# A hand-ordered kernel on one core: the opening fifth in another order, with alpha of chunk 0 loaded first

## The chip, the core and the metric

The kernel runs on one core of one Trainium2 chip. A core has four compute engines: TensorE (PE, matrix products and transposes into PSUM), VectorE (DVE), ScalarE (ACT) and GpSimd (POOL). A fifth one, SyncE (SP), here only issues the DMA transfers. Each engine works through a queue of its own in order, and waits on semaphores for what other engines or DMAs produce. The metric is the device time of one execution in microseconds (us); lower is better.

## The reference

```python
def _attn_ref(q, k, v, alpha):               # each (4, 8, 768, 48)
    for t in range(S):
        state = alpha[:, :, t, :, None] * state + np.einsum('bhd,bhe->bhde', k[:, :, t], v[:, :, t])
        y[:, :, t] = np.einsum('bhd,bhde->bhe', q[:, :, t], state)

x = attn_out.transpose(0, 2, 1, 3).reshape(3072, 384)
h = x @ w_in                                 # 384 x 2048
g = h * np.clip(h + 3.0, 0.0, 6.0) / 6.0
out = g @ w_out                              # 2048 x 384
```

The first half is a gated linear attention: a state of 48 x 48 per batch and head is decayed by alpha and updated at each of 768 positions. The second half is a feed-forward block with the hard-swish activation on the 3072 tokens. The two weight matrices come as float64.

## The kernel before

**Tiling.** The sequence is cut into chunks of 128 positions: 6 chunks for each of 4 batches, 24 in all, numbered j. Two chunks form a group g of 256 tokens. In a chunk the recurrence is turned into matrix products: products of alpha along the chunk scale k and q, and scores inside halves of 64 positions, together with a state carried between the halves, give y.

**Steps.** The program is a list of short words. Each word names a step and its arguments, and `run` calls them in the written order; each step's instructions go to the queue of their engine in that order. Nothing else sets the order. The words used below:

- `la.j`, `lk.j`, `lq.j` (line 251 for j under 6, line 262 from 6 on): SP loads alpha, k, q of chunk j. Up to chunk 5 they go into three ring buffers `rings`; from 6 on each load is four DMAs into the tiles `aq`, `kq`, `qq` (Python name `quads`), whose 16 padding columns are set by two POOL memsets (line 257) at the first use of each tile. `lv.j.z` (272): two DMAs that load v into buffer z.
- `w.i` (162, 166): SP loads slice i of the weights as float64, 768 KB, i from 0 to 7 of the first matrix and 8 to 15 of the second. `d1.i` (186), `d2.i` (196), `dx.i` (191) on ScalarE, `d3.i` (203, 205, or 207 to 210) on VectorE and `d4.i` (217) on POOL turn it to float32. Slices share five raw buffers: slices 0, 5, 8, 11, 14 the first, 1, 6, 9, 12, 15 the second, 2, 7, 10, 13 the third, 3 and 4 one each. A later load into a buffer waits for the `d4` of the earlier slice.
- `ta.j`, `tk.j`, `tq.j` (282): PE transposes into a PSUM bank (from chunk 6 on VectorE does it, 286). `ca.j` (300): copy of alpha, ScalarE. `r.j` (309, 313) and `p.j` (320): VectorE scans that give decay and growth. `k.j`, `q.j` (332): the scaled k and q.
- `kb.j` (374, PE) and `ck.j` (378, ACT): k by token. `u.j` (429, PE), `sm.j.b` (437, 439, DVE), `st.j` (409, POOL): the state. `sv.j.b` (419 on ACT; 415 on POOL where a batch starts), `qa.j.b` (366, ACT): state and q placed beside v and scores. `sc.j` (346, PE), `m.j` (356, DVE): scores and mask. `ya.j`, `yb.j` (455, PE), `cy.j` (464, ACT): y of both halves, kept as `xT`.
- `fa.i`, `fb.i` (489) and `f.g.i` (478): PE, hidden block i of group 0 in halves, or of a whole group; `fr` (494, ACT) and `fg` (498, DVE) apply the activation. `b.c.n` (516, PE): the second product for chunk c.
- `x`, `y` (537 to 541, 647), `xc`, `s`: VectorE sums of weights and inputs, with which groups from 2 on use fast matrix multiplication: `M.g.i` (600, PE) are products of the first matrix, `P.g.i` (703, PE) of the second, from group 1 on. `O`, `so`: stores, SP. `K`, `G`, `n`, `o`, `e`, `h`: copies and sums behind them.
- `z.m.n` (532): n matmuls of the identity on PE whose result nobody reads.

Each DMA of the SP queue waits, besides its buffers, for the eighth DMA before it. So at most eight are under way, and the loads follow each other in the order of their words.

Of the kernel before, what the change touches and what calls it, by code (L numbers as in the profile page):

```python
# [17 lines left out]
def kernel(  # L18
# [228 lines left out]

    def load_akq(name, j):
# [6 lines left out]
        if j < FIRST + NQ:  # L255
            for o in (BLK, 3 * BLK):
                nc.gpsimd.memset(to[o : o + BLK, :, V - 1, D - BLK : BLK], 1.0)
# [675 lines left out]
```

## Time and profile before

| | us |
|---|---|
| median of 3 runs | 534.24 (534.19 to 534.98) |
| the profiled execution, its time | 533.84 |
| its span in the profile | 531.8 |
| PE busy | 522.2 (98%) |
| DVE busy | 477.0 (90%) |
| ACT busy | 257.4 (48%) |
| POOL busy | 50.4 (9%) |

Times in a profile count from the start of the span. A row of a timeline has the start, the time from its first instruction's start to its last one's end, the engine, the line of the kernel, the operation, the tiles out<-in with shapes, the count of instructions, and in brackets the idle time of the engine before it with what ended it. A float32 matmul has two records, and the records of a row overlap: 24 records of 128x256 at line 478 take 5.45 us in one row, so 0.23 us each. A row of stretches has the length and then, for each engine, the busy time and the number of instructions, the granted TensorE clock, the mean busy share of the 16 DMA engines (sums of packet times, which can exceed 1) and GB/s. In a list of DMA issues the last column is the time from issue to landing.

### The profile page before, as it was taken

Reading aid. Unit: us, or ns where it says so; the run is one execution under the profiler, and the core shown is the slowest. Engines: PE = TensorE matmul, PEld = TensorE weight load, DVE = VectorE, ACT = ScalarE, POOL = GpSimd, SP = SyncE. Lnnn points to the kernel's source line nnn. Section 1 sums busy time; section 2 is a strip of 40 time slices with the busy share of each in tenths; the row PEclk is TensorE's granted clock in tenths of the full one; section 3 lists DMA queues with packets and bytes.
Section 4 is the critical chain, followed back from the end, with each engine's and each line's share of the span. In section 5 each row is a group of like instructions: output and inputs, shape, how many; then the busy total and the mean of one; then the engine's idle time right before and its main releaser. Section 6 shows DMA issues by size and latency. Waiting matters only on the chain.

```text
span 531.8 us, 15143 instructions
## 1 busy us (share of the span) xinstructions
PE 522.2 (98%) x6306; PEld 496.9 (93%) x6306; DVE 477.0 (90%) x849; ACT 257.4 (48%) x503; POOL 50.4 (9%) x71
## 2 busy tenths in 40 slices
...
DMA packets 124100, 54.40 MB, mean 102 GB/s; under 512 B 83328, under 2 KB 116864, under 8 KB 124032
## 3 DMA queue, kind: packets, MB, share of 16 engines
...
## 4 chain that ended last, share of the span: by engine, by line
PE 81%; DVE 9%; ACT 3%; DMA 3%; POOL 2%; issue 1%; SPq 0%; DVEq 0%; POOLq 0%; ACTq 0%
PE m_ps L703 34%; PE m_ps L600 34%; PE m_ps L478 4%; PE t_ps L455 3%; PE t_ps L346 2%; PE t_ps L429 2%; DMA v<-in_v_dram 1%; DMA raw<-in_moe_w_out_dram 1%; DVE rings L647 1%; DVE R L309 1%; DVE raw L537 1%; ACT raw L186 1%; DVE g_sb L647 1%; ACT raw L191 1%; DVE w L537 1%
## 5 line engine op out<-in xcount | busy, mean ns | idle before, releaser
L606 ACT COPY g_sb<-m_ps 128x512 f32<-128x512 f32 x110 | 63.6, 584 | 123.7 <-PE m_ps L600 104.3
L703 PE MATMUL m_ps<-w,g_sb 128*128 128x192 f32 x704 | 121.7, 327 | 0.0
L703 PEld LDWEIGHTS m_ps<-w,g_sb 128*128 128x128 f32 x704 | 113.7, 190 | 0.4
L703 PE MATMUL m_ps<-rings,g_sb 128*128 128x192 f32 x528 | 91.5, 326 | 0.0
L703 PEld LDWEIGHTS m_ps<-rings,g_sb 128*128 128x128 f32 x528 | 85.4, 190 | 0.1
L600 PE MATMUL m_ps<-xc,w 128*128 128x128 f32 x640 | 82.8, 277 | 0.4 <-DVE w L541 0.4
L600 PEld LDWEIGHTS m_ps<-xc,w 128*128 128x128 f32 x640 | 77.5, 192 | 1.7 <-issue 0.6
L494 ACT ACTIVATE r<-g_sb,half 128x512 f32<-128x512 f32 x80 | 56.8, 722 | 33.1 <-DVE g_sb L541 12.1
L498 DVE SCALAR_TENSOR_TENSOR g_sb<-r,g_sb 128x512 f32<-128x512 f32 x80 | 53.7, 683 | 4.3 <-ACT r L494 3.9
L600 PE MATMUL m_ps<-xT,raw 128*128 128x128 f32 x400 | 52.5, 277 | 0.0
L600 PEld LDWEIGHTS m_ps<-xT,raw 128*128 128x128 f32 x400 | 48.6, 192 | 0.6
L409 POOL TENSOR_TENSOR st<-sm,R 128x192 f32<-128x192 f32 x20 | 12.9, 643 | 352.2 <-DVE sm L439 305.5
L647 DVE TENSOR_TENSOR g_sb<-g_sb 128x512 f32<-128x512 f32 (+1 forms) x55 | 41.9, 792 | 0.2
L600 PE MATMUL m_ps<-xT,w 128*128 128x128 f32 x320 | 42.0, 276 | 0.0
L600 PEld LDWEIGHTS m_ps<-xT,w 128*128 128x128 f32 x320 | 39.3, 192 | 0.1
L366 ACT COPY A<-q 48x256 f32<-48x256 f32 x88 | 35.6, 404 | 5.0 <-DVE q L332 3.8
L356 DVE TENSOR_TENSOR A<-t_ps,mask 64x256 f32<-64x256 f32 x96 | 36.0, 413 | 0.4
L478 PE MATMUL m_ps<-xT,w 128*128 128x256 f32 x144 | 32.8, 382 | 0.1
L600 PE MATMUL m_ps<-xc,raw 128*128 128x128 f32 x240 | 31.8, 276 | 0.0
L309 DVE TENSOR_TENSOR_SCAN R<-t,ones 128x516 f32<-128x516 f32 x24 | 29.6, 1235 | 1.0 <-ACT t L300 0.9
L478 PEld LDWEIGHTS m_ps<-xT,w 128*128 128x128 f32 x144 | 26.7, 190 | 3.8 <-POOL w L217 0.2
L600 PEld LDWEIGHTS m_ps<-xc,raw 128*128 128x128 f32 x240 | 29.6, 192 | 0.1
...
## 6 DMA issues: line engine op xcount, KB each, us to landing
raw<-in_moe_w_out_dram SPq DMA_DIRECT2D x8, 768.0 KB, 5.3
raw<-in_moe_w_in_dram SPq DMA_DIRECT2D x6, 768.0 KB, 6.6
v<-in_v_dram SPq DMA_DIRECT2D x48, 96.0 KB, 3.1
out_dram<-oh SPq DMA_DIRECT2D x44, 96.0 KB, 1.7
...
aq<-in_alpha_dram SPq DMA_DIRECT2D x36, 96.0 KB, 2.7
qq<-in_q_dram SPq DMA_DIRECT2D x36, 96.0 KB, 2.5
```

What stands on the lines that cost most here:

```text
L309: nc.vector.tensor_tensor_scan(out=reverse(R, n - 1, n), data0=reverse(ax, n, n), data1=reverse(ones, n, n), initial=0.0, op0=ALU.mult, op ...
L356: nc.vector.tensor_tensor(out=to[:, a], in0=sc[a][half], in1=mask[half, half].unsqueeze(1).to_broadcast([HB, NP, HB]), op=ALU.mult)
L366: nc.scalar.copy(out=to[:, a], in_=Q_t[j][64 * a : 64 * a + D, :, half])
L409: nc.gpsimd.tensor_tensor(out=st, in0=sm, in1=R_t[j][:, :, 0:1].to_broadcast([C, NP, D]), op=ALU.mult)
L455: nc.tensor.matmul(y_of(j, (i + 1) // 2, p)[:, HB * b : HB * b + HB], vb[:, p, e : e + 32], A_t[j][:, b, 2 * p + a], start=(b == 0 and i = ...
L478: nc.tensor.matmul(h[:, f], w1[:, kk, o : o + C], xT_t[g][:, kk], start=(kk == 0), stop=(kk == KT - 1))
L494: nc.scalar.activation(out=to, in_=h, func=AF.Relu, bias=half, scale=1.0 / 6.0)
L498: nc.vector.scalar_tensor_tensor(out=to, in0=r, scalar=1.0, in1=h, op0=ALU.min, op1=ALU.mult)
L600: nc.tensor.matmul(acc[g][i][:, f * C : (f + 1) * C], spots[w][:, f * C : (f + 1) * C], x_of(g, x), start=(first and f == 0), stop=last, s ...
L606: nc.scalar.copy(out=slots[z], in_=acc[g][i])
L647: nc.vector.tensor_tensor(out=out, in0=in0, in1=in1, op=ALU.subtract)
L703: nc.tensor.matmul(to[g], a, rhs[:, f], start=(first and f == 0), stop=(last and f == HF - 1), skip_group_check=True)
```

## The change

The word list gets another order from its start up to the first products of group 2, a fifth of the span. The steps are the same, with two words more: `pd.0` and `pd.1` set the padding of the six tiles of one parity at once (six POOL memsets each); the loads `la`, `lk`, `lq` of chunks 6 and 7 no longer do it. Behind that, only `lv.12.1`, moved behind `kr.10`, differs; all later words stand as before.

Some of the moves: `la.0` is issued ahead of `w.0`; `ta.0.0` stands ahead of the eight fill matmuls `z.0.8`; `d2.0` and `d3.0` come behind `ca.0` and `r.0 p.0`. In SP's queue the first sixteen DMAs are the same ones in another order: before `w.0 la.0 lk.0 la.1 lq.0 lk.1 lv.0 (two) la.2 w.2 lq.1 lv.1 (two) lq.2 w.1 lk.2`, after `la.0 w.0 la.1 lk.0 la.2 lq.0 lv.0 (two) lk.1 w.2 lv.1 (two) lq.1 lq.2 w.1 lk.2`. POOL's queue begins, before, `sv.0.0 st.1 d4.2 d4.0 st.2 d4.1`, and after, `d4.0 sv.0.0 st.1 pd.0 st.2 d4.2 d4.1`. PE's steps up to `fa.2.0`, and again up to `M.2.0.2`, are the same set in both.

```diff
@@ -245,6 +245,11 @@
         b, c = divmod(j, NC)
         return t[b, :, c * C : (c + 1) * C, :]
 
+    def pad(r):
+        for name in "akq":
+            for o in (BLK, 3 * BLK):
+                nc.gpsimd.memset(quads[name, r][o : o + BLK, :, V - 1, D - BLK : BLK], 1.0)
+
     def load_akq(name, j):
         src = rows({"a": alpha, "k": k, "q": q}[name], j)
         if j < FIRST:
@@ -252,9 +257,6 @@
                               in_=src.rearrange("h s d -> s h d"))
             return
         to = quads[name, j % NQ]
-        if j < FIRST + NQ:
-            for o in (BLK, 3 * BLK):
-                nc.gpsimd.memset(to[o : o + BLK, :, V - 1, D - BLK : BLK], 1.0)
         to = to.rearrange("r p v d -> r p (v d)")
         t = src.rearrange("(p a) (u v) d -> a u p (v d)", a=2, v=V)
         for o in range(4):
@@ -727,7 +729,7 @@
 
     steps = {
         "la": lambda j: load_akq("a", j), "lk": lambda j: load_akq("k", j),
-        "lq": lambda j: load_akq("q", j), "lv": load_v, "w": load_weight,
+        "lq": lambda j: load_akq("q", j), "lv": load_v, "pd": pad, "w": load_weight,
         "d1": round_low, "d2": magnitude, "dx": sign, "d3": high_bits, "d4": add_low,
         "ta": lambda j, *i: transposed("a", j, *i), "tk": lambda j, *i: transposed("k", j, *i),
         "tq": lambda j, *i: transposed("q", j, *i), "ca": place_alpha, "r": decay, "p": growth,
-        run("""z.0.5 z.0.3 z.0.1 z.0.8 qa.0.0 w.0 d2.0 d3.0 la.0 ta.0.0 ca.0 r.0 lk.0 tk.0.1 k.0
-               z.0.2 p.0 la.1 ta.1.2 lq.0 tq.0.3 ca.1 r.1 lk.1 lv.0.0 sv.0.0 d1.0 kb.0.0 ck.0 z.0.2
-               u.0.2.1 sm.0.0 sv.0.1 q.0 qa.0.1 tk.1.0 k.1 p.1 z.0.2 sc.0.2.3 m.0 la.2 ta.2.0 ca.2
-               dx.0 w.2 d2.2 kb.1.0 ck.1 lq.1 r.2 sm.0.1 st.1 tq.1.2 q.1 d3.2 z.0.3 d1.2 dx.2 lv.1.1
-               u.1.3.1 sv.1.0 sm.1.0 p.2 sm.1.1 sc.1.0.2 m.1 ya.0.3 yb.0 cy.0 lq.2 w.1 d1.1 tq.2.1
-               q.2 d4.2 lk.2 tk.2.3 k.2 fa.2.0 d4.0 st.2 sc.2.0.2 d2.1 d3.1 m.2 dx.1 d4.1 qa.1.1
-               lk.3 la.3 ta.3.1 ca.3 la.4 fa.0.1 sv.1.1 w.3 r.3 ta.4.3 ca.4 r.4 tk.3.1 k.3 kb.2.0
-               qa.1.0 d2.3 ya.1.2 yb.1 cy.1 fa.1.2 lq.3 ck.2 d1.3 p.3 d3.3 lv.2.2 u.2.3.2 sm.2.0
-               d4.3 fb.2 tq.3.1 q.3 fb.1 qa.2.0 sm.2.1 sv.2.0 st.3 fr.0.2.0 fg.0.2 lk.4 tk.4.0
-               sv.2.1 w.5 d2.5 k.4 d3.5 d1.5 qa.3.0 d4.5 qa.2.1 sc.3.1.3 m.3 w.6 d2.6 d1.6 d3.6 d4.6
-               lv.3.0 lq.4 w.7 kb.3.2 fb.0 f.0.3.3 kb.4.0 ya.2.1 ck.3 u.3.3.2 sm.3.0 fr.0.3.1 fg.0.3
-               fr.0.1.0 fg.0.1 qa.3.1 sv.3.0 sm.3.1 p.4 d2.7 sv.3.1 d1.7 d3.7 d4.7 f.0.5.0 fr.0.5.1
-               fr.0.0.0 fg.0.5 fg.0.0 tq.4.3 ck.4 la.5 ta.5.2 f.0.6.3 ca.5 w.4 d2.4 ya.3.0 yb.3 cy.3
-               fr.0.6.1 yb.2 cy.2 w.9 d2.9 q.4 qa.4.1 d1.4 d1.9 dx.4 la.6 w.8 d3.4 r.5 lk.5 w.10
-               d3.9 p.5 ca.6 fg.0.6 d4.9 w.12 lq.5 lv.4.1 d2.8 d3.8 f.0.7.2 d1.8 st.4 d4.8 d4.4 w.11
-               fr.0.7.0 fg.0.7 f.1.7.0 fr.1.7.1 fg.1.7 sc.4.0.2 m.4 f.1.1.1 fr.1.1.0 fg.1.1 f.1.3.3
-               fr.1.3.1 d2.10 d1.10 tk.5.3 f.1.0.2 d2.12 d3.10 d4.10 w.13 fg.1.3 fr.1.0.0 fg.1.0 k.5
-               d3.12 lq.6 f.1.6.0 f.1.2.1 u.4.1.0 sm.4.0 d1.12 d4.12 sv.4.0 qa.4.0 ya.4.2 fr.1.6.1
-               fg.1.6 w.15 tq.5.3 fa.4.3 sv.4.1 d2.11 kb.5.1 d2.13 fr.1.2.0 f.1.4.2 fr.1.4.1 d1.11
-               sm.4.1 q.5 r.6 d3.11 d3.13 fg.1.4 d4.11 lv.5.0 lk.6 tq.6 p.6 d2.15 d3.15 fg.1.2 d1.13
-               d4.13 sc.5.0.3 yb.4 f.1.5.0 fr.1.5.1 fg.1.5 tk.6 m.5 b.1.0.2 fb.4 b.1.1 d1.15 d4.15
-               st.5 y.5 w.14 la.7 lk.7 cy.4 d2.14 qa.5.1 ck.5 b.0.0.1 fr.0.4.0 d3.14 k.6 q.6 ca.7
-               fg.0.4 d1.14 d4.14 x.0 y.1 y.10 b.0.1 y.0 y.2 u.5.2 P.1.0.0 K.1.0 qa.5.0 sv.5.0
-               qa.6.1 P.1.1.3 b.0.2 b.1.2 kb.6.0 ya.5.3 y.6 s.1.0.0 sm.5.0 sv.5.1 G.1.0.0 tk.7
-               s.1.1.1 s.1.2.3 x.1 yb.5 cy.5 b.1.3 sc.6.1.2 lv.6.2 ck.6 u.6.3.0 s.1.3.2 x.2 P.1.2
-               b.0.3 K.1.1 y.7 s.1.4 s.1.5 y.11 y.3 r.7 xc.2.1 x.3 y.4 y.8 xc.2.3 k.7 xc.2.0 xc.2.4
-               y.9 y.12 y.16 y.13 y.15 P.1.3.3 K.1.2 P.1.4 bo.1 P.1.5 xc.2.5 G.1.1.1 P.1.6 y.14 y.17
-               y.19 xc.2.6 sm.6.0 G.1.2.2 y.20 M.2.0.2 lv.12.1 la.8 O.1.1 O.1.0 ca.8 y.18 y.21 y.23
-               so.1 G.1.3.3 n.2.0.8 bo.0 lq.7 lv.7.0 O.1.2 m.6 xc.2.2 xc.2.10 xc.2.7 tq.7 r.8 p.7
-               xc.2.8 sv.6.1 M.2.15.3 M.2.1 kb.7.3 n.2.1.9 M.2.16 M.2.2 n.2.2.10 M.2.7.0 n.2.7.11
-               sm.6.1 xc.2.9 q.7 p.8 M.2.3 M.2.4 n.2.4.12 M.2.8 o.2.0.0 M.2.5 n.2.5.13 qa.7.0 sv.6.0
-               st.7 lk.8 O.1.3 lq.8 lk.9 la.9 la.10 tk.8 tq.8 lq.10 lq.9 ya.6.1 yb.6 M.2.9 z.1.3
 ...
+        run("""z.0.5 z.0.3 z.0.1 qa.0.0 la.0 w.0 ta.0.0 z.0.8 ca.0 d2.0 r.0 p.0 d3.0 la.1 lk.0
+               ta.1.2 tk.0.1 k.0 z.0.2 ca.1 r.1 d1.0 z.0.2 kb.0.0 ck.0 la.2 lq.0 tq.0.3 lv.0.0 lk.1
+               q.0 p.1 z.0.2 u.0.2.1 sm.0.0 tk.1.0 k.1 sc.0.2.3 ta.2.0 dx.0 qa.0.1 sv.0.1 ca.2 w.2
+               d2.2 sm.0.1 m.0 r.2 z.0.3 kb.1.0 ck.1 d1.2 lv.1.1 lq.1 u.1.3.1 tq.1.2 lq.2 w.1 lk.2
+               d4.0 sv.0.0 st.1 sv.1.0 dx.2 sm.1.0 d3.2 sm.1.1 q.1 p.2 ya.0.3 sc.1.0.2 m.1 yb.0
+               tq.2.1 q.2 la.3 w.3 lk.3 la.4 w.5 lq.3 lv.2.2 pd.0 st.2 d4.2 sv.2.0 cy.0 d1.1 tk.2.3
+               k.2 fa.2.0 sc.2.0.2 d2.1 d3.1 m.2 dx.1 d4.1 ta.3.1 fa.0.1 kb.2.0 qa.1.0 ca.3 qa.1.1
+               sv.1.1 r.3 tk.3.1 ya.1.2 yb.1 fa.1.2 ta.4.3 ck.2 cy.1 d2.3 p.3 k.3 d3.3 fb.2 tq.3.1
+               q.3 qa.2.1 d1.3 ca.4 u.2.3.2 d4.3 fr.0.2.0 fg.0.2 sm.2.0 sm.2.1 d2.5 d3.5 r.4 qa.3.0
+               d1.5 d4.5 st.3 w.6 d2.6 d1.6 lv.3.0 lk.4 w.7 lq.4 fb.0 sc.3.1.3 m.3 d3.6 f.0.3.3
+               tk.4.0 kb.3.2 fb.1 fr.0.3.1 ck.3 sv.2.1 u.3.3.2 sm.3.0 k.4 sm.3.1 fg.0.3 d2.7
+               fr.0.1.0 d1.7 qa.3.1 sv.3.0 qa.2.0 d3.7 p.4 f.0.5.0 tq.4.3 la.5 ta.5.2 kb.4.0 ck.4
+               sv.3.1 fr.0.5.1 ca.5 w.4 q.4 fg.0.5 fg.0.1 la.6 r.5 pd.1 d4.6 d4.7 f.0.6.3 ya.3.0
+               yb.3 ya.2.1 cy.3 fr.0.6.1 yb.2 w.9 d1.4 d2.4 cy.2 d1.9 d2.9 fr.0.0.0 dx.4 fg.0.6
+               d3.4 lv.4.1 lk.5 w.8 st.4 sc.4.0.2 f.0.7.2 f.1.7.0 fr.1.7.1 d2.8 m.4 d3.9 fg.0.0
+               d4.9 d4.4 fr.0.7.0 u.4.1.0 f.1.3.3 f.1.1.1 sm.4.0 ca.6 fg.0.7 fg.1.7 d3.8 f.1.0.2
+               tk.5.3 r.6 lk.6 w.10 w.12 lq.5 d2.10 d1.8 d4.8 fr.1.1.0 fg.1.1 d1.10 qa.4.1 lq.6
+               w.11 f.1.2.1 f.1.6.0 sv.4.0 fr.1.3.1 fr.1.0.0 d1.12 d2.12 tk.6 d3.10 d4.10 w.13
+               fg.1.0 f.1.4.2 sm.4.1 fg.1.3 d3.12 d4.12 fr.1.6.1 fa.4.3 d1.11 d2.11 fr.1.2.0 la.7
+               w.15 lv.5.0 k.6 k.5 fg.1.6 kb.5.1 fr.1.4.1 d2.13 sv.4.1 d3.11 fg.1.4 d4.11 fg.1.2
+               p.5 d3.13 d1.13 f.1.5.0 tq.5.3 q.5 fr.1.5.1 w.14 lk.7 ck.5 d2.15 qa.4.0 d3.15 d1.15
+               d4.15 qa.5.1 d2.14 b.0.0.1 fb.4 b.1.0.2 ya.4.2 yb.4 sc.5.0.3 ca.7 fg.1.5 d3.14 m.5
+               tq.6 d1.14 fr.0.4.0 cy.4 d4.14 d4.13 st.5 u.5.2 b.0.1 kb.6.0 P.1.0.0 b.1.1 tk.7
+               fg.0.4 p.6 P.1.1.3 s.1.0.0 q.6 sm.5.0 y.5 y.0 y.6 x.0 sv.5.1 qa.5.0 K.1.0 s.1.1.1
+               ck.6 sv.5.0 ya.5.3 yb.5 cy.5 sc.6.1.2 y.3 x.1 s.1.2.3 G.1.0.0 y.7 y.1 x.2 y.8 xc.2.1
+               s.1.3.2 y.2 y.9 y.11 s.1.4 xc.2.3 y.10 y.4 y.13 s.1.5 y.16 y.15 y.17 xc.2.4 xc.2.5
+               y.12 y.19 x.3 r.7 xc.2.6 la.8 lv.6.2 u.6.3.0 b.0.2 b.1.2 P.1.2 K.1.1 P.1.3.3 K.1.2
+               P.1.4 P.1.5 b.1.3 b.0.3 bo.1 G.1.1.1 k.7 P.1.6 sm.6.0 G.1.2.2 y.20 M.2.0.2 ca.8 y.18
+               y.21 y.23 xc.2.0 G.1.3.3 n.2.0.8 lq.7 O.1.2 O.1.0 so.1 bo.0 lv.7.0 m.6 xc.2.2
+               xc.2.10 xc.2.7 tq.7 y.14 r.8 p.7 xc.2.8 sv.6.1 M.2.15.3 M.2.1 kb.7.3 n.2.1.9 M.2.16
+               M.2.2 n.2.2.10 M.2.7.0 n.2.7.11 sm.6.1 xc.2.9 q.7 p.8 M.2.3 M.2.4 n.2.4.12 qa.6.1
+               M.2.8 o.2.0.0 M.2.5 n.2.5.13 qa.7.0 st.7 sv.6.0 O.1.3 lq.8 lk.9 lk.8 la.9 la.10 tk.8
 ...
```

172 lines of the change are left out of this document (87 added, 85 removed).

## The prediction

> **What bounds the kernel now.** I read the page's head and chain first, then the busy time by stretches, then the timelines of single queues in the opening.
>
> ```profile
> PE 522.2 (98%) x6306; PEld 496.9 (93%) x6306; DVE 477.0 (90%) x849; ACT 257.4 (48%) x503; POOL 50.4 (9%) x71
> ...
> PE 81%; DVE 9%; ACT 3%; DMA 3%; POOL 2%; issue 1%; SPq 0%; DVEq 0%; POOLq 0%; ACTq 0%
> ```
>
> Busy time in four stretches: before the first hidden-layer matmul, the crowded part, the rest of the reordered part, and everything behind it:
>
> ```profile
> core 0: us, PE busy (x) PEld busy (x) DVE busy (x) ACT busy (x) POOL busy (x), PEclk, DMA share, GB/s
> 0.00:24.94 24.94, 18.92 (x288) 16.49 (x288) 19.87 (x39) 14.82 (x21) 9.74 (x23) 1.00 1.11 198
> 24.94:50.64 25.70, 25.47 (x372) 22.71 (x372) 25.16 (x41) 24.12 (x46) 9.15 (x7) 1.00 0.95 241
> 50.64:127.47 76.83, 76.75 (x741) 62.89 (x740) 74.61 (x114) 35.90 (x62) 20.36 (x25) 1.00 0.51 128
> 127.47:531.80 404.33, 401.09 (x4906) 394.78 (x4906) 357.37 (x657) 182.55 (x379) 11.14 (x17) 1.00 0.36 83
> ```
>
> TensorE is the bound from 24.94 us on: it idles 0.23 us of the second stretch and 0.08 of the third. Before 24.94 it idles 6.02 us, and there the DMA share is 1.11: loads set the pace. In the second stretch VectorE (25.16 of 25.70) and ScalarE (24.12) run close behind it. So the reordering can gain three things: an earlier start of the dense part, the few waits inside it, and the wait at its end. It can lose at any point where TensorE runs dry. PE's own rows at these places:
>
> ```profile
> start us, us, engine line op out<-in xcount [idle before <-releaser]
> 1.47 6.67 PE L532 MATMUL m_ps<-ident 128*128 128x128 f32 x34 [1.47 <-POOL ident masks.py:199]
> 7.97 1.04 PE L282 MATMUL t_ps<-ident,rings 128*128 128x128 f32 x8
> ...
> 23.55 1.16 PE L282 MATMUL t_ps<-ident,rings 128*128 128x128 f32 x8 [0.29 <-DVE sm L439]
> 24.94 1.60 PE L489 MATMUL m_ps<-xT,w 128*128 128x128 f32 x12 [0.24 <-POOL w L217]
> ...
> 30.64 1.30 PE L455 MATMUL t_ps<-A,v 128*32 128x64 f32 x64 [0.23 <-ACT A L366]
> ...
> 127.89 1.13 PE L600 MATMUL m_ps<-xc,w 128*128 128x128 f32 x8 [0.42 <-DVE w L541]
> ```
>
> The row at 24.94 is `fa.2.0`, the first real work; the row at 127.89 is `M.2.1`, ahead of which PE waits 0.42 us for the VectorE sum `y.23`. `M.2.0.2` closes the same set of PE steps in both orders, so up to there no PE work is added or removed: only idle time can differ.
>
> **The change part by part.** First the loads. SP's issues, and then the time to landing of the loads 1, 2, 6, 9, 13 and 16 (input weights, alpha of chunk 0, k of 1, alpha of 2, second half of v of 1, k of 2):
>
> ```profile
> 0.75 0.44 SPq L162 DMA_DIRECT2D raw<-in_moe_w_in_dram  x1
> 1.25 0.47 SPq L251 DMA_DIRECT2D rings<-in_alpha_dram  x1
> ...
> 6.37 1.14 SPq L251 DMA_DIRECT2D rings<-in_k_dram  x1
> ...
> 9.45 0.62 SPq L251 DMA_DIRECT2D rings<-in_alpha_dram  x1
> ...
> 11.90 1.76 SPq L272 DMA_DIRECT2D v<-in_v_dram  x2
> ...
> 16.80 2.86 SPq L251 DMA_DIRECT2D rings<-in_k_dram  x2
> ```
>
> ```profile
> raw<-in_moe_w_in_dram SPq DMA_DIRECT2D x1, 768.0 KB, 5.0
> rings<-in_alpha_dram SPq DMA_DIRECT2D x1, 192.0 KB, 5.7
> ...
> rings<-in_k_dram SPq DMA_DIRECT2D x1, 192.0 KB, 5.6
> ...
> rings<-in_alpha_dram SPq DMA_DIRECT2D x1, 192.0 KB, 4.5
> ...
> v<-in_v_dram SPq DMA_DIRECT2D x1, 96.0 KB, 7.0
> ...
> rings<-in_k_dram SPq DMA_DIRECT2D x1, 192.0 KB, 6.9
> ```
>
> *`la.0` ahead of `w.0`, `ta.0` ahead of `z.0.8`.* Alpha landed at 1.25 + 5.7 = 6.95 and `ta.0` waited on to 7.97 behind 17 fill matmuls. Now it is issued at 0.75 and lands between 0.75 + 4.5 = 5.25 and 0.75 + 5.7 = 6.45; I take 5.25, since 768 KB less lie ahead of it. Nine fills take 9/17 of 6.67 = 3.5 us, done at 5.0. `ta.0` takes half of 1.04, then comes the copy `ca.0`; VectorE's and POOL's rows:
>
> ```profile
> 9.22 1.23 DVE L309 TENSOR_TENSOR_SCAN R<-t,ones 128x516 f32<-128x516 f32 x1 [0.94 <-ACT t L300]
> ...
> 11.17 1.22 DVE L320 TENSOR_TENSOR_SCAN P<-t 128x516 f32<-128x516 f32 x1
> ...
> 14.80 0.68 DVE L332 TENSOR_TENSOR k<-t_ps,R 128x512 f32<-128x512 f32 x1
> ...
> 18.07 1.23 DVE L309 TENSOR_TENSOR_SCAN R<-t,ones 128x516 f32<-128x516 f32 x1
> ...
> 20.41 0.71 DVE L203 TENSOR_SCALAR w<-w 128x768 f32<-128x768 f32 x1
> ...
> 25.56 0.68 DVE L332 TENSOR_TENSOR k<-t_ps,R 128x512 f32<-128x512 f32 x1
> ...
> 29.45 1.62 DVE L309 TENSOR_TENSOR_SCAN R<-t,ones 128x516 f32<-128x516 f32 x1
> ...
> 72.48 0.36 DVE L439 TENSOR_TENSOR s<-t_ps,st 128x192 f32<-128x192 f32 x1 [1.14 <-PE t_ps L429]
> ...
> 77.64 0.56 DVE L207 TENSOR_SCALAR w<-w 128x768 f32<-128x768 f32 x1
> ...
> 82.40 1.77 DVE L207 TENSOR_SCALAR w<-w 128x768 f32<-128x768 f32 x1
> ```
>
> ```profile
> 20.05 0.52 POOL L409 TENSOR_TENSOR st<-sm,R 128x192 f32<-128x192 f32 x1 [12.31 <-DVE sm L439]
> 22.84 3.88 POOL L217 TENSOR_TENSOR w<-w,raw 128x768 int32<-128x768 int32 x2 [2.27 <-ACT raw L191]
> 28.12 1.86 POOL L217 TENSOR_TENSOR w<-w,raw 128x768 int32<-128x768 int32 x1 [0.75 <-ACT raw L191]
> ...
> 52.27 0.56 POOL L257 MEMSET aq<- 32x64 f32 x2
> ```
>
> `ta.0` to `r.0` took 9.22 - 7.97 = 1.25 us, so `r.0` starts at about 5.25 + 1.25 = 6.5 instead of 9.22. VectorE has no other use for that time until data arrives, so not all of the 2.7 us count.
>
> *q of chunk 0 moves from fifth load to sixth.* The sixth landed at 6.37 + 5.6 = 11.97. By then `r.0`, `p.0`, `d3.0`, `k.0` and `r.1` fit in: from 6.5, two R scans and one P scan (3.7) with reciprocals, a weight step of two parts (0.71 each, row 20.41) and a product of 0.68: 6.0 with the short reciprocals. `q.0` starts at about 12.5, then `p.1` (1.22), `sm.0.0`, and `k.1` at about 14.5. Before, `k.1` started at 14.80 with `p.1` still to come behind it. VectorE's lead is 0.3 + 1.1 = 1.4 us.
>
> *v of chunk 1 moves ahead of q of chunk 1* (loads 11 and 12 instead of 12 and 13; the later half landed near 12.8 + 7.0 = 19.8, now about 18). `u.1` and `sm.1.0` can follow `r.2` without a gap, so the lead of 1.4 us is kept to `q.2`.
>
> *k of chunk 2 is load 16 in both orders, behind the same fifteen loads.* It landed at 16.80 + 6.9 = 23.70. `tk.2` and `fa.2.0` stand behind it in both, so `fa.2.0` can't start before 23.70 + 0.5 = 24.2. That caps the gain of the start at 24.94 - 24.2 = **0.75 us**, and `k.2` at 24.2 against 25.56 leaves VectorE ahead by 1.3.
>
> *POOL.* `d4.0` moves ahead of `sv.0.0` (d4.0 waits for `dx.0`; its reader `ya.0` runs past 20), and `pd.0` with six memsets (half of 0.56 each: 1.7 us) and `st.2` move ahead of `d4.2`. Cover: POOL waited 12.31 us for `sm.0.1`. `st.2` needs `sm.1.1`. `r.2` began at 18.07, now near 17; its scan, `sm.1.0` and the two parts of `d3.2` come first, so `sm.1.1` is near 20.2. `st.2` (0.52) and `d4.2` (half of 3.88), after `p.2` if that holds it up, end by 24.2. If that cover is gone, `fa.2.0` and, behind `sv.2.0` on ScalarE, `cy.0` are late together. `pd.1` stands between `st.3` and `d4.6`; between their producers on VectorE lie `d3.5`, `r.4`, `m.3` and `d3.6`, more than the 1.7 of the memsets: nothing. The six loads of `aq`, `kq`, `qq` that followed their memsets lose that wait; DMA is at 0.51 there, so nothing.
>
> *SP behind POOL.* `w.5` reuses the buffer of `w.0` and is asked for four places earlier; `d4.0`, now first on POOL, frees it in time. `w.6` waits for `d4.1` and holds `lv.3.0`, `lk.4`, `w.7`, `lq.4`, `la.5` and `w.4` behind it. `d4.1` ended at 28.12 + 1.86 = 29.98; with VectorE's lead it ends near 28.7. The first reader of these loads, `tk.4`, stands behind `fb.2`, `fb.0` and `f.0.3`, which follow `fa.1.2`, and that itself waits for `d4.1`; a load takes 5 to 7: nothing, but a late `d4.1` would be felt at `tk.4` one for one.
>
> *`qa.1.0` ahead of `ca.3` on ScalarE*: the 0.23 us before 30.64 go.
>
> *`u.4` ahead of four hidden-layer blocks*: VectorE's 1.14 us before 72.48 go; PE has none there, so this is lead for VectorE alone. `y.14` and `xc.2.0` move behind `y.23`: another 0.8. With 1.3 + 1.14 + 0.8, VectorE is some 3.2 us ahead at `y.23`, PE 1.0 ahead: the **0.42** before 127.89 go, with about 2 us to spare. `w.14` is asked for earlier relative to `d3.14`; VectorE may wait there up to 0.5, inside that margin.
>
> *`lv.12.1`, `O.1.1`, `qa.6.1` later*: their queues have room behind 127.47 (DMA 0.36, ACT 182.55 of 404.33). Nothing.
>
> Sum: -0.75 - 0.23 - 0.42 = **-1.40 us**, carried to the end because PE is dense behind 127.47. The profiled execution took 533.84, so 532.44; the median of the runs is 534.24, 0.40 above it, so **532.8 us** (-0.27%). A measurement of this kernel tells about 0.2% (1.07 us) from no change.
>
> [...] The scan of 1.62 at 29.45, against 1.23 and 1.22, lies beside the POOL step of 28.12 to 29.98; the step of 1.77 at 82.40 compares with 0.56. So a POOL weight step can hold up a VectorE step, here by up to 1.77 - 0.56 = 1.21 us. [...]
>
> **The rivals.** (a) *The lead is lost at `p.2`: no difference.* `d4.2` now becomes ready when `st.2` ends, about 0.2 us after `p.2` starts on VectorE. If it comes first, the scan waits up to 1.86 (the 28.12 row): the lead of 1.3 turns into -0.6, `k.2` and `sc.2` are no earlier than before, and only 0.42 is gained at most: 533.8. For it: the distance is small and the 29.45 row shows such a wait. Against: `p.2` comes first by the sums. The same time results if load 16 lands 0.75 later.
>
> (b) *VectorE falls behind POOL's weight steps in the crowded stretch: slower.* Five `d4` steps fall into it, VectorE has 0.54 us of slack there, and PE works directly behind it. Each block beyond those of before costs 1.2 to 1.86. One eats the gain; it decides from the second: 2 x 1.21 - 1.40 = +1.0, 535.3, and a third gives 536.5. For it: which `d4` step meets which scan is wholly new. Against: the rows of before show 0.4 (29.45) and 1.2 (82.40), not one at every pair.
>
> (c) *Larger gain.* If load 16 lands a microsecond earlier, the start follows VectorE's lead instead, 1.4 for 0.75: 532.2; if PE could also use the 1.14 us that VectorE wins at 72.48, 531.0.
>
> **How the numbers follow.** Forecast with (c) 0.54, (a) 0.21, (b) 0.25. The range goes from 531.0 (c) to 536.0 (between two and three blocks of b). Range of the forecast alone: 531.0 to 533.1. Faster 0.54, same 0.21, slower 0.25.
>
> **What would show it.** `r.0` starts at 6 to 7 instead of 9.22, `k.1` near 14.5, `fa.2.0` near 24.2, no wait before `M.2.1`, which starts near 126.5; PE idle between `fa.2.0` and `M.2.1` under 0.4. Wrong if alpha still lands near 7, if a scan beside a `d4` takes 2 to 3 us before 50, or if PE idles a microsecond at one place between 25 and 127.

## The result, and the profile after

The changed kernel takes 532.93 us (median of 10 runs, 532.32 to 533.67) against 534.11 us before (10 runs on the same chip, 533.33 to 534.98): a ratio of 0.9979, with an interval of 0.9969 to 0.9988. The forecast was 532.8 us, so the size was right. The way to it was not, and this section shows where the time lies. The profiled execution took 533.17 us (span 531.4) against 533.84 (531.8) before; it lies 0.24 above its median and the one before 0.27 below, which is why the two traces differ by 0.67 us and the medians by 1.18.

The head of the page after, and the head of its chain:

```profile
PE 522.0 (98%) x6306; PEld 498.0 (94%) x6306; DVE 475.8 (90%) x849; ACT 257.7 (48%) x503; POOL 51.8 (10%) x71
...
PE 86%; DVE 10%; ACT 1%; DMA 1%; issue 1%; POOL 0%; DVEq 0%; ACTq 0%; POOLq 0%
```

Busy time of the changed kernel in three stretches, cut at the start of `fa.2.0` and of `M.2.1`. The columns are the engines' busy time with instructions, then the granted PE clock, DMA share and GB/s:

```profile
0.00:24.90 24.90, 18.68 (x288) 16.59 (x289) 20.39 (x40) 15.50 (x23) 13.43 (x30) 0.97 1.11 213
24.90:127.31 102.41, 102.02 (x1114) 86.70 (x1113) 99.22 (x159) 58.39 (x101) 26.67 (x23) 0.99 0.61 153
127.31:531.40 404.09, 401.26 (x4908) 394.75 (x4906) 356.23 (x652) 183.81 (x381) 11.67 (x18) 1.00 0.37 83
```

`fa.2.0` starts at 24.90, where it started at 24.94 before: the opening gained nothing. `M.2.1` starts at 127.31 instead of 127.89, and what follows takes 404.09 against 531.80 - 127.89 = 403.91. The whole difference is made between 24.9 and 127.3, and the granted clock of 0.97 and 0.99 is new against the trace before. TensorE's rows at the places that the prediction showed:

```profile
5.46 0.99 PE L284 MATMUL t_ps<-ident,rings 128*128 128x128 f32 x4
...
21.99 0.69 PE L348 MATMUL t_ps<-q,k 48*64 48x64 f32 x32 [1.53 <-DVE q L334]
23.20 1.91 PE L284 MATMUL t_ps<-ident,rings 128*128 128x128 f32 x8
24.90 2.47 PE L491 MATMUL m_ps<-xT,w 128*128 128x128 f32 x12
27.30 0.69 PE L348 MATMUL t_ps<-q,k 48*64 48x64 f32 x32
...
30.72 1.10 PE L457 MATMUL t_ps<-A,v 128*32 128x64 f32 x64
...
88.39 0.56 PE L431 MATMUL t_ps<-v,kb 64*48 64x48 f32 x16 [0.39 <-ACT xT L466]
...
127.31 1.10 PE L602 MATMUL m_ps<-xc,w 128*128 128x128 f32 x8
```

The waits before `ya.1` (30.72) and `M.2.1` are gone. (`ya.1` is the step whose row stood at 30.64 before.) A new one of 0.39 stands before `u.5` at 88.39. `fa.2.0` takes 2.47 us for 1.60, and the clock says why (the same columns as above):

```profile
20.00:22.00 2.00, 0.47 (x34) 0.31 (x26) 1.93 (x5) 1.98 (x2) 0.49 (x1) 1.00 1.36 220
...
23.20:24.90 1.70, 1.70 (x14) 1.47 (x9) 1.66 (x5) 1.53 (x3) 1.65 (x1) 0.54 0.89 303
24.90:26.40 1.50, 1.50 (x8) 1.50 (x8) 1.50 (x3) 1.50 (x2) 0.00 (x0) 0.50 1.17 302
26.40:27.30 0.90, 0.90 (x8) 0.78 (x7) 0.83 (x2) 0.90 (x1) 0.00 (x0) 0.81 1.52 179
27.30:30.00 2.70, 2.70 (x52) 2.63 (x52) 1.91 (x5) 2.24 (x6) 1.86 (x1) 1.00 1.04 299
```

TensorE is busy for only 0.47 of the two microseconds from 20 to 22, and some time later its clock is halved for about 3.4 us (23.3 to 26.7), just when the dense part begins. In the trace before, it was busy for 1.21 of these two and kept the full clock (1.00). TensorE never stands for more than 1.56 us at a time here; what sets the clock back, the trace doesn't show.

The half clock is no fixed property of either order. A mean granted clock of 0.997 over the whole span is half clock for some 3 us (an estimate, 0.003 x 531.4 / 0.5 = 3.2; the profiled run, with 0.997, shows the 3.4 above). Six of the ten runs of the changed kernel have 0.997 or less (median 532.94 us), four have 1.00 (532.73 us). In the three later measurements of the kernel before, 8, 10 and 11 of 27 runs have 0.997, and their medians lie 0.3 to 0.4 us above those of the runs at 1.00.

VectorE and POOL in the opening:

```profile
7.11 1.23 DVE L311 TENSOR_TENSOR_SCAN R<-t,ones 128x516 f32<-128x516 f32 x1 [2.93 <-ACT t L302]
...
15.10 0.68 DVE L334 TENSOR_TENSOR k<-t_ps,R 128x512 f32<-128x512 f32 x1
17.61 1.54 DVE L311 TENSOR_TENSOR_SCAN R<-t,ones 128x516 f32<-128x516 f32 x1
...
21.97 1.23 DVE L322 TENSOR_TENSOR_SCAN P<-t 128x516 f32<-128x516 f32 x1
...
25.26 0.68 DVE L334 TENSOR_TENSOR k<-t_ps,R 128x512 f32<-128x512 f32 x1
```

```profile
21.51 0.51 POOL L411 TENSOR_TENSOR st<-sm,R 128x192 f32<-128x192 f32 x1 [2.33 <-DVE sm L441]
22.12 2.73 POOL L217 TENSOR_TENSOR w<-w,raw 128x768 int32<-128x768 int32 x1
```

Load 16 (k of chunk 2), its issue and, in the view of the DMAs, its time to landing:

```profile
16.16 0.49 SPq L256 DMA_DIRECT2D rings<-in_k_dram  x1
```

```profile
rings<-in_k_dram SPq DMA_DIRECT2D x1, 192.0 KB, 7.0
```

`r.0` starts 2.1 us earlier than before. At `k.1` 0.84 us of lead is left (15.10 for 14.80, but with the 1.14 us of `p.1` already done), and at `k.2` 0.30 (25.26 for 25.56). `d4.2`, which `fa.2.0` needs, runs from 22.12 to 24.85: it takes 2.73 us beside the scan `p.2`, where `d4.1`, with no scan beside it here, takes 1.86.

The balance from `fa.2.0` to `M.2.1`: before, 127.89 - 24.94 = 102.95, of it 0.23 + 0.42 idle, so 102.30 of work. After, 102.41, of it 0.39 idle and 0.86 of half clock (`fa.2.0` to `sc.2` is 2.40 us for 1.54), so 101.16 of work. Without the idle time in the brackets, **the same steps take 1.14 us less**. That is a term which the prediction held to be zero. (0.44 of it will turn out, under `x_merge`, to be waiting that the brackets don't count.)

### The profile page after: what moved, and what is told of

Its sections match the earlier page's. It is cut to its first block, busy times and chain, and to the rows that moved or that the text cites. A ratio compares the mean times of both kernels' runs of the same rounds, so it can differ in the third digit from the quotient of the medians.

```text
span 531.4 us, 15123 instructions
## 1 busy us (share of the span) xinstructions
PE 522.0 (98%) x6306; PEld 498.0 (94%) x6306; DVE 475.8 (90%) x849; ACT 257.7 (48%) x503; POOL 51.8 (10%) x71
## 4 chain that ended last, share of the span: by engine, by line
PE 86%; DVE 10%; ACT 1%; DMA 1%; issue 1%; POOL 0%; DVEq 0%; ACTq 0%; POOLq 0%
PE m_ps L705 38%; PE m_ps L602 35%; PE t_ps L457 4%; PE m_ps L518 3%; PE t_ps L348 2%; PE t_ps L431 2%; DVE g_sb L500 1%; DVE R L311 1%; DMA raw<-in_moe_w_out_dram 1%; DVE w L207 1%; DVE w L208 1%; PE m_ps L534 1%; DVE raw L210 1%; DVE A L358 1%; PE t_ps L284 1%
## 5 line engine op out<-in xcount | busy, mean ns | idle before, releaser
L322 DVE TENSOR_TENSOR_SCAN P<-t 128x516 f32<-128x516 f32 x24 | 29.7, 1239 | 0.2
```

The lines of the kernel that those rows point to most:

```text
L322: nc.vector.tensor_tensor_scan(out=P_t[j], data0=aX[j % 2][:, 0:n], data1=ini[j % 2], initial=0.0, op0=ALU.mult, op1=ALU.add)
```

## The experiments

All ratios are against the kernel before on the same chip; times of different runs come from different chips, on which the kernel before has medians of 533.6 to 534.1 us. The labels in the headings are those of the runs. In the diffs only the order of words changes, where nothing else is said.

### The two halves of the change: x_open, x_rest

```diff
 x_open: the words up to fa.2.0 in the changed order,
-the rest in the changed order
+the rest in the order before (pd.1 ahead of la.7)
 x_rest: the words up to fa.2.0 in the order before,
-the rest in the order before
+the rest in the changed order
```

> Edit: the order of after up to and with fa.2.0, then all remaining words in the order of before (pd.1 ahead of la.7). Theory (the terms add up: start of the dense part and waits behind it): the start's part alone, fa.2.0 a few tenths of a us earlier, and M.2.1 still waits about 0.4 for y.23; 0.2 to 0.75 us below before, ratio 0.9986 to 0.9996. Rival 1 (the opening's lead is swallowed, since VectorE and ScalarE pace the stretch from 25 to 50 us): ratio 1.000. Rival 2 (it is all the opening): ratio 0.998.

> Edit: the order of before up to and with fa.2.0, then the remaining words in the order of after. Theory: the waits behind the start go (0.42 ahead of M.2.1, 0.23 inside) but the start stays at 24.9; 0.65 us below before, ratio 0.9988. Rival 1 (opening's lead swallowed): the whole gain is here, ratio 0.9979. Rival 2 (all the opening): ratio 1.000.

`x_open`: 534.84 us, 1.0020 (1.0011 to 1.0029). `x_rest`: 537.59 us, 1.0069 (1.0057 to 1.0082). Each half alone makes the kernel slower, though both together make it faster; none of the outcomes that were expected came. One row of each says why. TensorE of `x_open`:

```profile
34.19 0.71 PE L431 MATMUL t_ps<-v,kb 64*48 64x48 f32 x32 [0.90 <-DMA v<-in_v_dram]
```

ScalarE and then TensorE of `x_rest`:

```profile
28.23 0.71 ACT L421 COPY v<-st 48x192 f32<-48x192 f32 x2 [3.50 <-POOL st L411]
```

```profile
32.44 1.11 PE L376 MATMUL t_ps<-ident,k 128*128 128x128 f32 x4 [3.56 <-DVE A L358]
```

In `x_open` the loads come in one order and are used in the other, and `u.2` waits 0.90 us for v of chunk 2. `fa.2.0` started at 24.63, but the wait of 0.42 before `M.2.1` was still there, and the work of the stretch was 102.4 us, as before. In `x_rest`, `sv.2.0` on ScalarE waits 3.50 us for `st.2`. POOL reaches `st.2` behind `d4.2` and `d4.0`, as it did before, and here behind the memsets of `pd.0` too (1.1 us more); but in the changed order `sv.2.0` stands much earlier in ScalarE's queue than in the order before. The weight steps queued behind `sv.2.0` come late, VectorE waits for them, the mask `m.2` with it, and TensorE stands for 3.56 us. So the gain can't be split between the halves by these runs: what they show is that a step placed for one order costs microseconds in the other.

### Alpha first: x_w0, x_la0

```diff
 x_w0: the changed kernel
-z.0.5 z.0.3 z.0.1 qa.0.0 la.0 w.0 ta.0.0
+z.0.5 z.0.3 z.0.1 qa.0.0 w.0 la.0 ta.0.0
 x_la0: the kernel before
-z.0.5 z.0.3 z.0.1 z.0.8 qa.0.0 w.0 d2.0 d3.0 la.0 ta.0.0 ca.0 r.0
+z.0.5 z.0.3 z.0.1 qa.0.0 la.0 w.0 ta.0.0 z.0.8 ca.0 d2.0 r.0 d3.0
```

> Edit: after with w.0 issued ahead of la.0 again, nothing else. Theory (alpha first lets r.0 and p.0 run before data for the rest is there): r.0 starts about 1 us later than the 7.11 of after, k.1 about 0.8 later than 15.10, and 0.3 to 0.8 us of the gain go: ratio 0.9985 to 0.9995. Rival (loads 9 to 16 pace the opening, whatever comes first): same as after, ratio 0.998.

> The kernel before, with the head of the changed order alone: la.0 ahead of w.0, ta.0 and ca.0 ahead of the eight fill matmuls, d3.0 behind r.0. The prediction's first term, as it stood: r.0 near 7, VectorE ahead by over a microsecond, fa.2.0 at 24.2, 0.75 us less, ratio 0.9986. What the changed kernel's trace suggests in its place: r.0 near 7, but k, q and v of chunk 0 land no earlier, so the lead is spent in waits for loads by 15 us; fa.2.0 within 0.3 us of 24.94, ratio 1.000.

`x_w0`: 534.17 us, 1.0006 (0.9997 to 1.0015); by the medians all that the change gained is gone. `x_la0`: 533.47 us, 0.9995 (0.9987 to 1.0004); no difference. VectorE, then TensorE of `x_w0`:

```profile
8.12 1.23 DVE L311 TENSOR_TENSOR_SCAN R<-t,ones 128x516 f32<-128x516 f32 x1 [3.94 <-ACT t L302]
...
16.11 0.68 DVE L334 TENSOR_TENSOR k<-t_ps,R 128x512 f32<-128x512 f32 x1
```

```profile
26.58 1.64 PE L491 MATMUL m_ps<-xT,w 128*128 128x128 f32 x12
```

In the changed order a load of alpha that comes 1.01 us later (`r.0` at 8.12 for 7.11) is handed on to `k.1` in full (16.11 for 15.10) and to `fa.2.0` with more (26.58 for 24.90). The 0.67 on top is the half clock: TensorE takes 3.55 us from `sc.1` to `fa.2.0` (23.03 to 26.58, granted clock 0.57 from 23.2 to 25.0 and 0.50 from 25.0 to 26.4), and 2.92 at full clock in `x_fill` below, 0.37 of them waiting for `d4.2`. In `x_w0` `d4.2` ended at 25.89, 1.04 later than in the changed kernel, so that at full clock `fa.2.0` would have been about a microsecond late (an estimate from these rows). The runs agree: nine of the eleven have a granted clock of 0.994 to 0.997 and a median of 534.36 us, the two others (0.999 and 1.00) took 533.06 and 533.09. So part of this loss is the clock and not alpha. In the old order the same two words bring `r.0` to 7.01, but VectorE gives the lead back at once:

```profile
13.78 0.36 DVE L437 COPY s<-t_ps 128x192 f32<-128x192 f32 x1 [0.94 <-PE t_ps L429]
...
14.65 0.68 DVE L332 TENSOR_TENSOR k<-t_ps,R 128x512 f32<-128x512 f32 x1
```

It waits 0.94 us at `sm.0.0` for `u.0`, `k.1` starts at 14.65 for 14.80, and `fa.2.0` at 24.79 for 24.94. Loading alpha first is thus worth nothing by itself. It is needed by the changed order, which puts `p.0`, `r.1` and `p.1` into the first microseconds and has no gap left to absorb a late alpha; how much of the time at the end hangs on it at full clock, two runs can't tell.

### The half clock: x_fill

```diff
 the changed kernel
-ya.0.3 sc.1.0.2
+ya.0.3 z.0.5 sc.1.0.2
```

> Edit: after with five fill matmuls (z.0.5) ahead of sc.1.0.2, in the 1.5 us in which PE idled before 21.99. Theory (PE's idle stretch made the granted clock fall to 0.5 between 23.2 and 27.3, and that cost some 0.8 us there): the clock stays at 1.00 there, fa.2.0's row takes 1.5 to 1.6 instead of 2.47, and the time is 0.4 to 0.8 us below after, ratio to before 0.9964 to 0.9972. Rival (the slow stretch is swallowed by waits behind it, or falls elsewhere): clock 1.00, but ratio 0.998 as after. If the fills hold up sc.1, 0.2 us are lost.

532.77 us, 0.9981 (0.9972 to 0.9990), against 532.93 us and 0.9979: no difference that can be told. The five fill matmuls do what they should; the clock stays at 1.00 in all eleven runs, `fa.2.0` starts at 24.99 and takes 1.60 again. But of the 0.86 us saved, TensorE gives 0.49 back at `u.5`:

```profile
24.99 1.60 PE L491 MATMUL m_ps<-xT,w 128*128 128x128 f32 x12 [0.37 <-POOL w L217]
...
88.11 0.56 PE L431 MATMUL t_ps<-v,kb 64*48 64x48 f32 x16 [0.88 <-ACT xT L466]
...
127.03 1.10 PE L602 MATMUL m_ps<-xc,w 128*128 128x128 f32 x8
```

`u.5` writes the PSUM bank that `cy.4` on ScalarE must read first, and `cy.4` comes by other engines' work. With a slow clock in the opening the wait is 0.39, without it 0.88. The row at 24.99 also shows what binds the start of the dense part: TensorE is ready and waits 0.37 us for `d4.2`.

### The wait before M.2.1: x_y14

```diff
 the kernel before
-xc.2.3 k.7 xc.2.0 xc.2.4 ... P.1.6 y.14 y.17 ... y.23 so.1 ... tq.7 r.8
+xc.2.3 k.7 xc.2.4 ... P.1.6 y.17 ... y.23 xc.2.0 so.1 ... tq.7 y.14 r.8
```

> The order before with y.14 and xc.2.0 behind y.23, nothing else. The prediction's third term: the wait of 0.42 before M.2.1 goes, 0.4 us faster than before, ratio 0.9992, M.2.1 at 127.47. Rival: VectorE is late at y.23 for other reasons too, the wait stays at 0.2 or more, ratio 1.000.

533.75 us, 1.0003 (0.9995 to 1.0012). In its trace the wait before `M.2.1` is gone, and a wait stands 6.5 us later, before a product that needs one of the sums that now come behind `y.14`. TensorE, then `y.23` on VectorE:

```profile
25.47 1.54 PE L489 MATMUL m_ps<-xT,w 128*128 128x128 f32 x12
...
127.56 1.10 PE L600 MATMUL m_ps<-xc,w 128*128 128x128 f32 x8
...
134.02 1.13 PE L600 MATMUL m_ps<-xc,raw 128*128 128x128 f32 x8 [0.41 <-DVE xc L539]
```

```profile
126.63 0.69 DVE L541 SCALAR_TENSOR_TENSOR w<-w 128x512 f32<-128x512 f32 x1
```

The move doesn't account for all of it. `y.23` starts 0.42 us earlier than before (126.63 for 127.05), but in this execution the clock was halved in the opening (0.53 from 22 to 24, 0.62 from 24 to 26), and TensorE itself is 0.46 later from `sc.2` on (26.94 for 26.48). What would be left of the wait at full clock, this run doesn't show. VectorE has the same work to do either way. In the changed kernel `y.23` starts at 124.61, 2 us ahead of what `M.2.1` needs, and no wait follows: the third term needs VectorE's lead, not only the place of `y.14`.

### Small tiles between large ones: x_split, x_unjoin, x_merge, x_join

If the 1.14 us are work, they have to lie in how TensorE's steps stand beside each other. Between `fa.2.0` and `M.2.1` the kernel before has 12 separate groups of steps with small tiles (`sc` 48x64, `u` 64x48, `ya` and `yb` 128x32) between full 128x128 ones; the changed kernel has 9.

```diff
 x_split: the changed kernel, nine pairs behind M.2.1 pulled apart, such as
-u.21.3.0 ... sc.21.1.2 ... M.9.6.0
+u.21.3.0 ... M.9.6.0 sc.21.1.2
 x_unjoin: x_fill
-sc.4.0.2 f.0.7.2     sc.5.0.3 ... u.5.2 b.0.1     u.6.3.0 b.0.2
+f.0.7.2 sc.4.0.2     sc.5.0.3 ... b.0.1 u.5.2     b.0.2 u.6.3.0
 x_merge: x_y14
-ya.2.1 ck.3 ... yb.2 ... f.0.7.2 ... sc.4.0.2     yb.5 cy.5 b.1.3 sc.6.1.2 lv.6.2 ck.6 u.6.3.0
+ck.3 ... ya.2.1 yb.2 sc.4.0.2 ... f.0.7.2     yb.5 cy.5 sc.6.1.2 lv.6.2 ck.6 u.6.3.0 b.1.3
 (q.4 is written ahead of sc.4; the order on VectorE stays)
 x_join: x_u5 (below), ya.6 yb.6 moved behind M.2.13 to ya.7, ya.20 yb.20 to ya.21
```

> Theory T (tile shapes): TensorE loses time at every group of small-tile steps (48x64, 64x48, 128x32 tiles) that stands alone between full 128x128 ones. From the start of fa.2.0 to M.2.1 the kernel before has 12 such groups and 102.3 us of work without its idle time, the changed kernel 9 and 101.1 to 101.2, so 0.3 to 0.4 us for each group, and this is the gain that the sum of the prediction didn't have. Here nine pairs of sc and u behind M.2.1 are pulled apart by one dense step; up to M.2.1 nothing is moved. T: 9 x 0.2 to 0.4 = 1.8 to 3.6 us slower than the changed kernel, 534.7 to 536.5, with TensorE busy all the time. Theory I (idle time, as the prediction had it: the same steps are the same work): within 0.5 us of the changed kernel's 532.9, and if it is slower, then by idle time on TensorE that the profile shows.

> The kernel with the five fill matmuls, and on TensorE three moves alone: f.0.7 ahead of sc.4, u.5 behind b.0.1, u.6 behind b.0.2. Between fa.2.0 and M.2.1 there are 12 separate groups of small-tile steps again, as before the change, where the parent has 9. Theory T, with the 3.18/9 = 0.35 us per group that the pulled-apart pairs gave: the stretch without its idle time takes 101.2 + 3 x 0.35 = 102.2 us; the wait of 0.88 before u.5 goes (bank 2 has long been read by then); M.2.1 at 127.0 to 127.4, the time 532.6 to 533.2. Theory I: the stretch without idle time stays at 101.2 and M.2.1 comes at 126.2, the time 531.9.

> The order before with the y14 edit, and on TensorE three moves alone: sc.4 behind yb.2, ya.2 next to yb.2, b.1.3 behind u.6; two groups of small tiles fewer, the order of all other engines stays. T: M.2.0 starts 0.5 to 0.8 us earlier than 125.52, and the time is 0.4 to 0.8 us below that of the y14 edit alone (VectorE may eat some of it at y.23). I: M.2.0 at 125.5 or later, the same time as with y14 alone.

> The kernel with u.5 on bank 1, and two groups of small tiles joined to others behind M.2.1: ya.6, yb.6 next to ya.7, and ya.20, yb.20 next to ya.21 (cy.6, cy.20, qa.8.1, xc.10.2 and xc.10.0 go along). Theory T: 2 x 0.35 = 0.7 us less than u.5 on bank 1 alone, 531.2 if that gives 531.9. Theory I: no difference between the two, or a new idle time at the later steps.

`x_split`: 536.03 us, 1.0045 (1.0032 to 1.0057), 3.1 us above the changed kernel (3.5 by the ratios). `M.2.1` starts at 127.25 as it did, the span ends at 534.5, so the rest takes 407.25 for 404.09: 3.16 us for nine groups, **0.35 us each**, and TensorE's rows behind 130 show no wait. (The same rest takes 403.9 to 404.1 in the ten traces with none of the edits of `x_split`, `x_join` and `x_y14`.) One of the pairs, in the changed kernel and then in `x_split`:

```profile
255.88 1.95 PE L602 MATMUL m_ps<-xT,w 128*128 128x128 f32 x16
257.76 0.57 PE L431 MATMUL t_ps<-v,kb 64*48 64x48 f32 x32
258.15 0.66 PE L348 MATMUL t_ps<-q,k 48*64 48x64 f32 x32
258.75 1.16 PE L602 MATMUL m_ps<-xc,w 128*128 128x128 f32 x8
259.74 2.77 PE L705 MATMUL m_ps<-rings,g_sb 128*128 128x192 f32 x16
```

```profile
256.55 1.95 PE L602 MATMUL m_ps<-xT,w 128*128 128x128 f32 x16
258.43 0.57 PE L431 MATMUL t_ps<-v,kb 64*48 64x48 f32 x32
258.94 1.16 PE L602 MATMUL m_ps<-xc,w 128*128 128x128 f32 x8
260.02 0.69 PE L348 MATMUL t_ps<-q,k 48*64 48x64 f32 x32
260.65 2.87 PE L705 MATMUL m_ps<-rings,g_sb 128*128 128x192 f32 x16
```

From the first row to the last it is 3.86 us together and 4.10 apart, and the full-tile step behind the second small one takes longer as well (2.87 for the 2.77 of the same sixteen behind a full-tile step). These rows put a price on pulling such a pair apart; what TensorE does in that time, they don't show.

`x_unjoin`: 532.91 us, 0.9989 (0.9981 to 0.9998). `fa.2.0` 24.97, `M.2.1` 126.97, with a wait of 0.37 in between: 101.63 us of work. The same order with its pairs together and no wait (`x_u5`, below) takes 125.93 - 24.98 = 100.95. Three groups cost 0.68, or 0.23 each. Rows of `x_unjoin`, then `M.2.1` of `x_u5`:

```profile
51.95 2.83 PE L480 MATMUL m_ps<-xT,w 128*128 128x256 f32 x12 [0.37 <-DVE g_sb L500]
...
126.97 1.10 PE L602 MATMUL m_ps<-xc,w 128*128 128x128 f32 x8
```

```profile
125.93 1.10 PE L602 MATMUL m_ps<-xc,w 128*128 128x128 f32 x8
```

`x_merge`: 534.22 us, 1.0010 (1.0002 to 1.0019), against the 533.75 of `x_y14` on the same chip. From `ya.1` to `M.2.1` it takes 96.15 us without its waits, against 96.46 for `x_y14`: two groups fewer save 0.31, 0.15 each, but `u.6`, now 2.4 us earlier, waits 0.47 for `ck.6`, and nothing is left.

The brackets make a wait too cheap, though. Where TensorE doesn't wait, the same two rows follow each other at the same distance in all these traces, to within 0.02 us; so what a wait costs can be read from the starts. The row ahead of `M.2.1` starts 0.89 us before it in the changed kernel and in `x_y14`, and 1.48 before it in the kernel before: the wait of 0.42 cost 0.59. By the same reckoning the wait of 0.23 at `ya.1` cost 0.50 (0.30 ahead of it, and 0.20 in its own row, which takes 1.30 in the five traces with this wait and 1.10 in those with no wait near it), two waits too short for a bracket 0.21 together (the rows at 37.13 and 50.64, which are followed 0.06 and 0.15 later than in `x_y14`), and the new wait of 0.39 at `u.5` 0.60. That is 0.65 more than the brackets before, 0.21 more after. So 0.44 of the 1.14 us are waits as well, and 0.70 is work. `x_unjoin` gives 0.62 for its three groups when its wait is counted so (0.43 for 0.37), and `x_merge` 0.49 for its two (0.65 for 0.47). TensorE does lose time at each such group, 0.2 to 0.35 us by these three runs, and the three groups fewer of the changed order account for nearly all of the 0.70.

`x_join` tried to draw gain from it behind `M.2.1`: 534.05 us, 1.0004 (0.9995 to 1.0013), 2.3 us slower than its parent. (Its `ya.20` reads the buffer of v behind the load of chunk 22, so y of chunk 20 is computed from other data; the work is the same.) `M.2.1` comes at 126.02, and after it TensorE stands 0.53, 0.68, 0.31 and 0.21 us at four places, among them:

```profile
134.44 1.16 PE L602 MATMUL m_ps<-xc,w 128*128 128x128 f32 x8 [0.53 <-DVE g_sb L539]
146.69 0.68 PE L348 MATMUL t_ps<-q,k 48*64 48x64 f32 x28 [0.68 <-issue]
```

Without these 1.73 us the rest would take 404.55 for the 404.07 of its parent; since a bracket counts less than the wait costs, this doesn't tell whether the work became less. Joining two groups by moving them microseconds away from their place cost more in waits than it saved here, 2.3 us net.

### Two steps further: x_best, x_u5

```diff
 x_best: x_fill, and
-pd.0 st.2 d4.2 sv.2.0 cy.0     u.5.2
+pd.0 d4.2 cy.0 st.2 sv.2.0     u.5.1
 x_u5: x_fill, and
-u.5.2
+u.5.1
```

> The changed kernel with the five fill matmuls ahead of sc.1, d4.2 ahead of st.2 on POOL (st.2 and sv.2.0 behind cy.0), and u.5 on bank 1 in place of bank 2, for which it waited 0.88 us at 88.11. Theory D: the start of fa.2.0 (24.99) is bound by d4.2, which lay beside p.2 and took 2.73 for 1.86; ahead of st.2 it ends near 22.9 and fa.2.0 starts at 24.1 to 24.3, so 0.7 us less, with 0.88 less at u.5: M.2.1 near 125.5, some 531.3 us, 0.9955 of before. Rival: p.2 is now the one that is held up, by up to 0.9 us, q.2, k.2 and sc.2 come as much later, and TensorE waits for them between 25 and 31 what it won; then only the 0.88 are left, 531.9.

> The kernel with the five fill matmuls, and u.5 on bank 1, which ck.5 has freed, in place of bank 2, which cy.4 must read first: nothing else. The wait of 0.88 us at 88.11 goes; VectorE is over 1 us ahead at y.23. M.2.1 at 126.2, 0.9 us less: 531.9, ratio 0.9965. Rival: y.23 or another VectorE step then ends last, and the wait comes back before M.2.0 or M.2.1, the same 532.8.

`x_best`: 533.75 us, 1.0003 (0.9994 to 1.0012). `d4.2` starts at 22.09 although `st.2` no longer stands ahead of it:

```profile
22.09 2.58 POOL L217 TENSOR_TENSOR w<-w,raw 128x768 int32<-128x768 int32 x1 [3.19 <-ACT raw L191]
```

It had been waiting for `dx.2` on ScalarE all along, and still meets `p.2` (which started at 21.79). `fa.2.0` gains 0.26 us (24.73 for 24.99). `st.2` now comes at 24.63, `sv.2.0` behind it on ScalarE at 25.18, and the weight step and the mask `m.2` queued behind that are 1.7 us later:

```profile
30.23 0.66 PE L376 MATMUL t_ps<-ident,k 128*128 128x128 f32 x4 [1.35 <-DVE A L358]
```

So both forecasts missed (531.3, and 531.9 of the rival). The rival was right that the gain at `fa.2.0` would be lost again, but not in the cause, since ScalarE and not `p.2` was held up, nor in the size: `M.2.1` comes at 127.87, later than the 127.03 of `x_fill`, though the 0.88 at `u.5` is gone.

`x_u5`: **531.77 us**, 0.9963 (0.9950 to 0.9977), the fastest of all, 1.0 us below `x_fill` as expected. `u.5` starts at 87.04 with no wait, `M.2.1` at 125.93, 1.10 earlier than in `x_fill`: the wait of 0.88 cost 1.10. From 25 us to the end no row of TensorE shows a wait.

## Why the prediction was right, and where it was wrong

The number was right by 0.1 us, with steps wrong in opposite directions. Its terms against the two traces, up to `M.2.1`, each wait at what it cost by the starts of the rows:

| term | forecast | measured |
|---|---|---|
| start of `fa.2.0` | -0.75 | -0.04 |
| half clock at the start of the dense part | not seen | +0.86 |
| waits before `ya.1` and `M.2.1` | -0.23 - 0.42 | -0.50 - 0.59 |
| two short waits of the trace before | not seen | -0.21 |
| new wait before `u.5` | "under 0.4" allowed, 0 in the sum | +0.60 |
| work of the same TensorE steps | 0 | -0.70 |
| sum | -1.40 | -0.58 |

The traces of two single executions thus differ by less than the medians do (1.18), and what makes up the rest can't be read from them. Runs of the changed kernel spread over 1.35 us, so the agreement to a tenth of a microsecond is partly luck.

- *Alpha and `r.0`*: right in kind. `ta.0` began at 5.46, `r.0` at 7.11 against "6 to 7". The transposes took 0.99 us from their start, where half of 1.04 was put.
- *VectorE's lead of 1.4 us at `k.1`*: 0.84. `k.1` came at 15.10, not 14.5; the scan `r.2` then took 1.54 beside `st.1`, and by `k.2` 0.30 was left.
- *"Load 16 caps the start at 24.2"*: this step failed. The load was issued at 16.16 and landed 7.0 us later at 23.16, earlier than thought, but it was not what bound the start. `d4.2` was to "end by 24.2"; it ended at 24.85. It could not start before 22.04, when `dx.2` on ScalarE ended, which the prediction didn't follow; by then `p.2` had come first (21.97), and POOL's step took 2.73 for 1.86. Rival (a) had named this meeting and the loss of the lead; only it expected the scan to be the one that waits. And `x_la0` shows the same lead lost at another place, in the old order. The term of 0.75 was worth 0.04. Rival (a) was thus nearer to what happened in the opening than the forecast was, though its time of 533.8 was not.
- *"No PE work is added or removed: only idle time can differ"*: this step failed too, and together with waits that cost more than their brackets (1.09 for 0.65) it saved the sum. The order of TensorE's steps alone moves their time: 0.70 us here; nine groups pulled apart cost 3.16 us without one wait (`x_split`).
- *The clock*: the prediction saw 1.00 in all stretches before and took it to stay. The half clock cost the profiled run 0.86 us at `fa.2.0`; `x_fill`, which avoids it, is not measurably faster, because most of it comes back as a wait before `u.5`. The four runs of the changed kernel at 1.00 (532.73) are not clearly faster than its six others (532.94) either.
- *The wait before `M.2.1`*: right, and with the 2 us to spare that were forecast. `x_y14` adds that the moved sums gain nothing by themselves. `M.2.1` came at 127.31 and not "near 126.5", since the start term was missing.
- *The moved POOL steps and rival (b)*: no scan of the changed kernel took over 1.57 us, and VectorE was never the one that TensorE waited for between 25 and 127. A hold of 1.86 us, the price in rival (a) and the upper one in rival (b), is the length of a weight step and was the author's estimate; no run shows a scan held up for so long. The longest scan beside a weight step took 1.62 us for 1.23 (29.45, in the kernel before), and there the step of 1.77 for 0.56 at 82.40 ran beside one from 81.73 to 83.75. The memsets of `pd` cost nothing in the changed order: behind them POOL still waits for VectorE, 2.33 us before `st.2` and 1.04 before `d4.6`. In `x_rest`, with `st.2` behind them and behind `d4.0`, they take 1.1 of the 3.50 us that `sv.2.0` waits; the cover that the prediction named for them was real.
- *SP*: the loads held no engine up in the changed kernel. In `x_open` one did, for 0.90.

What stays open: what decides in which execution the clock is halved, what it costs `x_w0` in the end, and how much of the wait before `M.2.1` the moved sums would take at full clock.
